# Weight signs through ScalarE's leaky slope, the first loads on one queue, and the big chunks' softmax and maxima spread over three blocks

## The chip, the cores and the metric

The kernel runs on one core of a Trainium2 chip. The metric is the device time of one execution, in microseconds (us). The engines are named as in the profile: PE (TensorE), PEld (its weight loads), DVE (VectorE), ACT (ScalarE), POOL (GpSimd), SP (the queue from which most transfers are issued; SPq and ACTq are the issuing sequencers of SP and ACT).

## What is computed

```python
w = softmax(weight_gen)                      # (4, 4096, 8 heads, 7 taps)
x_pad = 6 rows of zeros ahead of x           # x is (4, 4096, 192)
out = einsum('bshk,bskhg->bshg', w, x_unf)   # 7 taps of x, weighted per head
x = out.reshape(16384, 192)
h = x @ w_in                                 # w_in (192, 2048), float64
g = h * (1.0 / (1.0 + np.exp(-h)))
return (g @ w_out).astype(np.float32)        # w_out (2048, 192), float64
```

## The kernel before

Each of 128 partitions holds 128 consecutive tokens; four of them (TB) from every partition make a **block** of 512 tokens, so there are 32 blocks, 0 to 31. x and weight_gen come in **chunks** of 1, 1, 2 and then seven times 4 blocks; chunks 3 to 9, the big ones, begin at blocks 4, 8, ..., 28. For a block the seven taps are multiplied and added (`prep_steps`, L418 and L424, on DVE with a share on POOL), split into two float16 halves `xs` (L393 on ACT, L396 on DVE), transposed by a DMA into `xt` (L403) and copied with the two halves of the partitions swapped into `xu` (L388). Then come two products: `mm1` (L509) makes `h` for a pair of 128 columns of w_in at a time, ACT applies silu and makes the upper half of `g` (L521, L522), DVE the lower half (L527, `lower`), and `mm2` (L541) adds to `acc`. Eight pairs make a block. `mm1` runs three pairs ahead of `mm2`; four buffers hold `h`, so `mm1` of a pair waits until DVE has finished `lower` of the pair two before.

Before a chunk can be used, its weights need the softmax (`softmax_steps`: row maxima `wm` L318, subtraction L321 on POOL, exp L325 on ACT, row sums `ws` L329, their reciprocal L333 and L334, product L337 on POOL) and x needs the largest magnitude of the chunk, from which its float16 scale is taken (`scale_steps`: up to four partial maxima `xm` L351, their maximum `m_x` L157, a write of 128 values to DRAM, `d_x` L160, and a read back to all partitions, `mb_x` L161, `ra_x` L166 and the small scales).

Blocks 0 and 1 are an opening of its own. Block 0 runs in float32: its seven products are added up on PE (L455), turned on PE (L471), and `mm1` (L497) and `mm2` (L550) use the weights as float32. w_in and w_out arrive as pairs of 32-bit words (`raw`, nine buffers) and are turned to float32 in 8 + 8 pieces I0 to I7 and O0 to O7 (`convert_steps`): `move` (L211, ACT) shifts the exponent of the upper words, `sign` (L173 and L216, DVE) puts together the sign bit and the three bits of the lower words, and `join` (L220, DVE) combines them. `size` (L225, ACT) takes each piece's sum of magnitudes; the largest of the sums (`w_scale_steps`: L254 on DVE, a product on PE L257, L260 on DVE, a product L264) sets the weights' float16 scale, with which `upper_w` (L238) and `lower_w` (L242) make the float16 halves that block 1 is the first to use. The scale of block 1's x goes through PE (`x1_all`, L647, L660, L661), that of blocks 2 and 3 (chunk 2) through `x2_size` (L666) and `d_x`, `mb_x` on SP; `z2` is the step that reads them.

The order of all this is a table. `OPENING` has for each of the first 16 pairs three lists of steps (before `mm1`; after it; inside the `mm2` that follows): S, J stand for `sign`, `join` of an I piece and G, Q of an O piece, I and O for `move`, B and D for `size`, U, L, P, R for `upper_w` and `lower_w`, M and A for block 1's products and sums, X for its split and transpose, Wr, Wa, Wb, Wc for the weights' scale. `START` has the units at which the later steps are issued: a block has 16 units, two for each pair, and `chain` counts from two blocks before the block or chunk in question. DVE, ACT, PE and SP each execute in the order that results.

```python
    "any_s": (3, 3, 7, 9, 9, 9),
    "any_x": (1, 5, 6.5, 9, 9.5, 19.75, 19.75, 20.5),
    "any_v": (12, 13, 15, 19, 20, 20.75, 21.5, 22.25, 24.5, 25, 25),
```

Of the kernel before, what the change touches and what calls it, by code (L numbers as in the profile page):

```python
# [52 lines left out]
    "chunk2": (2.5,),  # L53
# [16 lines left out]
def kernel(  # L70
# [77 lines left out]
    def absmax_by_dma(m, name, queue=nc.sync):  # L148
# [20 lines left out]
        return got, [rows, over]  # L169
# [33 lines left out]
    wsum = const.tile([P, 2, NP], F32, name="wsum")  # L203

    def convert_steps(kind, p):
# [17 lines left out]
        def size():  # L223
            junk = sm_p.tile([P, 2 * D], mybir.dt.bfloat16, tag="junk", name=f"junk{kind}{p}", bufs=1)
            nc.scalar.activation(out=junk, in_=v, func=AF.Abs, accum_out=wsum[:, col, p:p + 1])  # L225

        return [move, sign, join, size]
# [46 lines left out]
    def load_x(c):  # L274
# [4 lines left out]
        if t0 == 0:  # L279
# [5 lines left out]
            nc.scalar.dma_start(out=t[1:1 + cut, 0:HALO, :], in_=xf[0:cut, T - HALO:T, :])  # L285
            nc.scalar.dma_start(out=t[1 + cut:P, 0:HALO, :], in_=xf[cut:P - 1, T - HALO:T, :])
# [312 lines left out]
    with tc.manual_schedule():  # L599
        load_w(0)  # L600
        load_x(0)
        load_w(1, nc.scalar)
        load_w(2, nc.scalar)
# [5 lines left out]
        load_x(1)  # L609
        load_piece("I", 1)  # L610
# [68 lines left out]
        step |= {"y": lambda: x_scales({"all": px[:, P:P + 1]}, 1), "x2": x2_size, "n2": lambda: (tot2(), rec2(), norm2()), "n1": lambda: (tot1(), rec1(), norm1()),  # L679
                 "Wr": w_rows, "Wa": w_turn, "Wb": w_over, "Wc": w_scale}  # L680
        for p in range(NP):
            for kind, names in (("I", "ISJ" "B" "UL"), ("O", "OGQ" "D" "PR")):
                steps = conv[kind, p] + [lambda k=kind, p=p: upper_w(k, p), lambda k=kind, p=p: lower_w(k, p)]
                step.update({f"{n}{p}": f for n, f in zip(names, steps)})
        for n in ("I0", "S0", "J0"):
            step.pop(n)

        for c in range(2, NC):
# [8 lines left out]
            def prepare(c=c, u0=u0):  # L697
# [122 lines left out]
```

## Time and profile before

| what | value |
|---|---|
| median of 3 runs | 1084.42 us (1084.2 to 1084.54) |
| the profiled execution | 1084.3 us, its span 1082.5 us |
| PE | 1049.9 us busy, 97% of the span |
| DVE, ACT | 784.7 us (72%), 775.0 us (72%) |
| POOL | 293.2 us (27%) |
| chain that ended last | PE 77%, DVE 9%, ACT 6%, DMA 5%, issue 3% |

The profile covers one execution. A busy share is a mean over stages that have different limits, so the table alone doesn't say where time can be won: a stage's waits do. Times of the span count from its start.

### The profile page before, as it was taken

How to read it: one execution, taken by the hardware profiler on the slowest of the kernel's cores; microseconds unless marked ns; L12 is line 12 of the kernel's file. 1: busy time of each engine (PE TensorE's matmuls, PEld its weight loads, DVE VectorE, ACT ScalarE, POOL GpSimd, SP SyncE). 2: the span in 40 equal slices, each digit the busy share in tenths (PEclk: the TensorE clock that was granted, in tenths of full speed). 3: DMA queues.
4: the chain of work that ended last, by engine and by line, in shares of the span. 5: the costliest groups of instructions: out<-in, count | busy, mean ns of one | idle time of the engine just before them, and what ended most of it. 6: DMA issues, size and time to landing. Idle time of an engine off the chain costs nothing.

```text
span 1082.5 us, 36860 instructions
## 1 busy us (share of the span) xinstructions
PE 1049.9 (97%) x16472; PEld 811.3 (75%) x16472; DVE 784.7 (72%) x1134; ACT 775.0 (72%) x1264; POOL 293.2 (27%) x169
## 2 busy tenths in 40 slices
PE   6988999999999999999999998999999999999998
PEld 4655677777777777777777776777777777777776
DVE  6888886678866697677867686667886669767643
ACT  3765777678777777777767785767877777777775
POOL 1000343331513343312433304333151334331100
PEclk9999999999999999999999999999999999999999
DMA  8412132111411115111331104111131111211110
GB/s 214 139 30 118 42 133 50 39 45 32 131 46 45 39 38 145 32 31 46 91 85 46 46 19 142 39 39 46 31 131 46 45 38 40 48 31 32 45 46 16
DMA packets 73790, 67.71 MB, mean 63 GB/s; under 512 B 52639, under 2 KB 67103, under 8 KB 72606
## 3 DMA queue, kind: packets, MB, share of 16 engines
q1 hardware_dynamic: 73184, 64.43, 21.8%
q8 instruction: 128, 2.10, 0.9%
q10 hardware_dynamic: 446, 0.93, 0.3%
q14 instruction: 32, 0.26, 0.1%
HBM read 28.37 MB, written 12.59 MB: 38 GB/s over the span
## 4 chain that ended last, share of the span: by engine, by line
PE 77%; DVE 9%; ACT 6%; DMA 5%; issue 3%; SPq 0%; DVEq 0%; ACTq 0%
PE h L509 37%; PE acc L541 37%; DVE pr L424 2%; ACT h L521 2%; DVE g L527 1%; PE acc L554 1%; DVE pr L418 1%; DMA xc<-in_x_dram 1%; DMA xu<-xt 1%; DMA xt<-xs 1%; DVE xm L351 1%; ACT g L522 1%; DMA d_x<-xs 1%; PE sum L455 1%; PE h L497 1%
## 5 line engine op out<-in xcount | busy, mean ns | idle before, releaser
L527 DVE SCALAR_TENSOR_TENSOR g<-h,gup,g 128x512 f16<-128x512 f32 x496 | 369.0, 747 | 264.8 <-ACT g L522 264.4
L541 PE MATMUL acc<-wo,g 64*128 64x192 f16 x11424 | 556.6, 243 | 0.0
L541 PEld LDWEIGHTS <-g 64*128 64x128 f16 x11424 | 528.5, 94 | 25.2 <-issue 0.2
L521 ACT ACTIVATE h<-h,inv 128x512 f32<-128x512 f32 x496 | 326.5, 658 | 251.0 <-PE h L509 250.2
L509 PEld LDWEIGHTS <-w 64*128 64x128 f16 x4464 | 278.7, 94 | 203.4 <-issue 24.0
L522 ACT ACTIVATE g<-h,gup 128x512 f16<-128x512 f32 x496 | 341.0, 687 | 16.2
L509 PE MATMUL h<-xt,w 64*128 64x512 f16 x2232 | 310.7, 376 | 10.8 <-DVE g L527 10.8
L509 PE MATMUL h<-xu,w 64*128 64x512 f16 x2232 | 308.8, 377 | 4.3 <-DMA xu<-xt 4.3
L418 POOL TENSOR_TENSOR pr<-xc,wc 128x768 f32<-128x768 f32 x87 | 144.4, 1674 | 507.5 <-DVE pr L424 407.2
L418 DVE TENSOR_TENSOR pr<-xc,wc 128x768 f32<-128x768 f32 x130 | 130.9, 1008 | 0.0
L424 DVE TENSOR_TENSOR pr<-pr,pr 128x768 f32<-128x768 f32 x128 | 130.1, 1016 | 0.3
L424 POOL TENSOR_TENSOR pr<-pr,pr 128x768 f32<-128x768 f32 x58 | 122.2, 2107 | 4.5
L575 DVE SCALAR_TENSOR_TENSOR o<-acc,od,t 128x192 f32<-128x192 f32 x120 | 44.1, 408 | 3.5 <-ACT t L574 3.5
L574 ACT ACTIVATE t<-acc,od 128x192 f32<-128x192 f32 x120 | 43.6, 418 | 3.8 <-PE acc L554 3.8
L321 POOL TENSOR_TENSOR wc<-wc,wm 128x896 f32<-128x896 f32 x7 | 12.3, 1757 | 107.6 <-DVE wm L318 107.6
L396 DVE SCALAR_TENSOR_TENSOR xs<-pr,xup,xs 128x768 f16<-128x768 f32 x31 | 35.3, 1138 | 6.4 <-ACT xs L393 4.3
L337 POOL TENSOR_TENSOR wc<-wc,ws 128x896 f32<-128x896 f32 x7 | 12.3, 1754 | 89.6 <-DVE ws L334 89.6
L393 ACT ACTIVATE xs<-pr,xup 128x768 f16<-128x768 f32 x31 | 28.7, 925 | 9.1 <-DVE pr L424 9.1
L351 DVE TENSOR_REDUCE xm<-xc 128x1 f32<-128x960 f32 (+1 forms) x28 | 34.4, 1228 | 0.0
L550 PEld LDWEIGHTS acc<-v_out,g 128*128 128x128 f32 x128 | 21.4, 196 | 4.9 <-issue 1.8
L550 PE MATMUL acc<-v_out,g 128*128 128x192 f32 x128 | 24.3, 344 | 0.0
L554 PEld LDWEIGHTS <-g 128*128 128x128 f16 x240 | 20.1, 100 | 5.4 <-issue 5.1
(87 smaller groups left out, 254.6 us busy)
## 6 DMA issues: line engine op xcount, KB each, us to landing
xc<-in_x_dram SPq DMA_DIRECT2D x7, 2112.0 KB, 10.4
xu<-xt SPq DMA_DIRECT2D x62, 192.0 KB, 2.8
out_dram<-o SPq DMA_DIRECT2D x58, 192.0 KB, 1.9
wc<-in_weight_gen_dram SPq DMA_DIRECT2D x7, 448.0 KB, 6.4
rawI<-in_moe_w_in_dram SPq DMA_DIRECT2D x16, 192.0 KB, 6.5
rawO<-in_moe_w_out_dram SPq DMA_DIRECT2D x8, 384.0 KB, 4.3
xc<-in_x_dram SPq DMA_DIRECT2D x1, 1344.0 KB
xc<-in_x_dram SPq DMA_DIRECT2D x2, 384.0 KB, 6.0
```

The lines of the kernel that those rows point to most:

```text
L351: nc.vector.tensor_reduce(out=m[:, i:i + 1], in_=x_t[c][:, cuts[i]:cuts[i + 1], :].rearrange("p t d -> p (t d)"), op=ALU.max, axis=AX.X, a ...
L396: nc.vector.scalar_tensor_tensor(out=xs[:, ts, D:2 * D], in0=acc, scalar=sc[c, "up"], in1=xs[:, ts, 0:D], op0=ALU.mult, op1=ALU.subtract)
L418: eng.tensor_tensor(out=pr[k].rearrange("p t (h g) -> p (t h) g", g=G), in0=xin, in1=wv, op=ALU.mult)
L424: eng.tensor_tensor(out=pr[k], in0=pr[k], in1=pr[l], op=ALU.add)
L509: nc.tensor.matmul(h_t[b, p + NP * i], w16[rows, g, part, p * P:(p + 1) * P], x_in[rows, :, k, :], start=n == 0, stop=n == NT9 - 1)
L521: nc.scalar.activation(out=h, in_=h, func=AF.Silu, scale=sc[c, "inv"])
L522: nc.scalar.activation(out=gh, in_=h, func=AF.Copy, scale=sc[c, "gup"])
L527: nc.vector.scalar_tensor_tensor(out=gl_t[b, f], in0=h, scalar=sc[chunk_of[b], "gup"], in1=gh_t[b, f], op0=ALU.mult, op1=ALU.subtract)
L541: nc.tensor.matmul(acc_t[b, i, t // 2][:, t % 2, :], g[rows, t * P:(t + 1) * P], wo16[rows, f, part], start=f == ORDER[0] and t % 2 == 0 a ...
L550: nc.tensor.matmul(acc_t[b, 0, t // 2][:, t % 2, :], gh_t[b, f][:, t * P:(t + 1) * P], v_out[:, f % NP, f // NP], start=f == 0 and t % 2 = ...
L574: nc.scalar.activation(out=t1, in_=a[0], func=AF.Copy, scale=sc[c, "od"])
L575: nc.vector.scalar_tensor_tensor(out=o[:, t, :], in0=a[1], scalar=sc[c, "od"], in1=t1, op0=ALU.mult, op1=ALU.add)
```

## The change

- `move` uses ACT's leaky slope (Prelu) in place of a copy: for negative values the slope of -2^32 raises the exponent by 32, and after the shift by three bits in `join` that is the sign bit. So `sign` shrinks to `rest`, one instruction (L174 in the new numbering), and the instruction at L216 is gone, once for each of 16 pieces.
- `size_w` takes the magnitudes of two pieces at once: eight instructions of 768 elements in place of 16 of 384.
- The rows of x ahead of block 0 and the weights of chunks 1 and 2 are loaded by SP's queue, not ACT's, in the order w of chunk 0, x of chunk 0, rows ahead, w of chunk 1, piece I0, x of chunk 1, w of chunk 2.
- Softmax of chunks 1 and 2 goes in between block 0's products; the scales of block 1 and of chunk 2 go through DRAM by POOL's queue, each a `d_x` and an `mb_x`, and `z2` moves from the 11th to the 14th pair.
- `Wa`, the product on PE that needs all sizes, moves from inside `mm2` of pair 3 to after it; `n1`, M and A move to earlier pairs.
- From chunk 4 on, the chunk's softmax and maxima begin up to 40 units earlier than before and lie in three blocks; chunk 3 has lists of its own.

```diff
 OPENING = (
...
-    ("I7 O6 B3", "O7 D2 D3 B4 B5 S6 J6 G4 Q4 G5 Q5 M5 A5", ""),
-    ("B6 D4", "D5 B7 S7 J7 G6 Q6 G7 Q7 M4 A4", ""),
-    ("", "D6 D7 Wr M3 A3", "Wa M2 A2"),
-    ("Wb M1 A1 M0 A0 X", "Wc U0 L0 U1 U2 P0 L1", "L2 U3 R0 P1 L3"),
+    ("I7 O6", "O7 B1 D1 B2 S6 J6 G4 Q4 G5 Q5 M4 A4 y", "M3 A3"),
+    ("D2", "S7 J7 G6 Q6 G7 Q7 B3 M2 A2", ""),
+    ("", "D3 M1 A1 Wr M0 A0 X", ""),
+    ("Wa", "Wb", "Wc U0 U1 P0 L0 L1"),
...
-    "any_s": (3, 3, 7, 9, 9, 9),
-    "any_x": (1, 5, 6.5, 9, 9.5, 19.75, 19.75, 20.5),
+    "first_s": (1, 1, 5, 8, 9, 9),
+    "first_x": (0, 3, 6, 11, 11.25, 15, 21, 21, 22),
+    "any_s": (-32, -32, -21, -15.5, -14.5, -14.5),
+    "any_x": (-38, -30.5, -22, -6, -5, 0, 4, 4, 5),
+    "early": (-40,),
...
         def move():
-            nc.scalar.activation(out=v, in_=raws[kind, p][..., 1].bitcast(F32), func=AF.Copy, scale=REBIAS)
-
-        def sign():
-            low, high = raws[kind, p][..., 0], raws[kind, p][..., 1]
-            bits(t, low, 29, ALU.logical_shift_right)
-            nc.vector.scalar_tensor_tensor(out=t, in0=high, scalar=SIGN, in1=t,
-                                           op0=ALU.bitwise_and, op1=ALU.bitwise_or)
+            nc.scalar.activation(out=v, in_=raws[kind, p][..., 1].bitcast(F32), func=AF.Prelu, scale=REBIAS,
+                                 alpha=TO_BIT_31)
+
+        def rest():
+            bits(t, raws[kind, p][..., 0], 29, ALU.logical_shift_right)
...
-            nc.scalar.dma_start(out=t[1:1 + cut, 0:HALO, :], in_=xf[0:cut, T - HALO:T, :])
-            nc.scalar.dma_start(out=t[1 + cut:P, 0:HALO, :], in_=xf[cut:P - 1, T - HALO:T, :])
+            nc.sync.dma_start(out=t[1:1 + cut, 0:HALO, :], in_=xf[0:cut, T - HALO:T, :])
+            nc.sync.dma_start(out=t[1 + cut:P, 0:HALO, :], in_=xf[cut:P - 1, T - HALO:T, :])
...
-        load_w(1, nc.scalar)
-        load_w(2, nc.scalar)
+        load_w(1)
...
-        px = ps_o.tile([P, 2, D], F32, tag="acc", name="x1_all").rearrange("p a d -> p (a d)")
+        got1, (rows_1, spread1, over1) = absmax_by_dma(xs1, "x1", nc.gpsimd)
+        rows_1()
+        spread1()
...
-            got, (rows, over) = absmax_by_dma(xs2, "x2")
+            got, (rows, spread, over) = absmax_by_dma(xs2, "x2", nc.gpsimd)
             rows()
+            spread()
```

The start of ACT's program. Before, four transfers are issued ahead of the first table load (`xc` is x, `wc` the softmax weights, the number is the buffer's):

```order
L285 DMA xc_114<-in_x_dram 112x1152
L286 DMA xc_114<-in_x_dram 15x1152
L307 DMA wc_119<-in_weight_gen_dram 128x224
L307 DMA wc_121<-in_weight_gen_dram 128x448
L623 ACT_TABLE_LOAD
L623 ACTIVATE warm<-ones 1x1
L325 ACTIVATE wc_112<-wc_112 128x224
```

Now:

```order
L625 ACT_TABLE_LOAD
L625 ACTIVATE warm<-ones 1x1
L327 ACTIVATE wc_112<-wc_112 128x224
L296 ACTIVATE xc_114<-zero 1x1152
L327 ACTIVATE wc_119<-wc_119 128x224
```

The four transfers have left ACT's order; they are in SP's, and ACT begins with its table.

DVE in the opening, up to the maximum of the weights' sizes (`w_rows`), which PE's `Wa` waits for. Before, the last pieces and three of block 1's sums (`pr`) stand ahead of it, each piece with three instructions:

```order
L173 TENSOR_SCALAR tI_304<-rawI_165 128x384
L216 SCALAR_TENSOR_TENSOR tI_304<-rawI_165,tI_304 128x384
L220 SCALAR_TENSOR_TENSOR v_in<-v_in,tI_304 128x384
L173 TENSOR_SCALAR tO_311<-rawO_170 128x384
L216 SCALAR_TENSOR_TENSOR tO_311<-rawO_170,tO_311 128x384
L220 SCALAR_TENSOR_TENSOR v_out<-v_out,tO_311 128x384
...
L418 TENSOR_TENSOR pr_2_352<-xc_114,wc_119 128x768
L424 TENSOR_TENSOR pr_0_350<-pr_0_350,pr_2_352 128x768
L254 TENSOR_REDUCE w_rows<-wsum 128x2
```

Now:

```order
L174 TENSOR_SCALAR tI_295<-rawI_165 128x384
L219 SCALAR_TENSOR_TENSOR v_in<-v_in,tI_295 128x384
L174 TENSOR_SCALAR tO_302<-rawO_170 128x384
L219 SCALAR_TENSOR_TENSOR v_out<-v_out,tO_302 128x384
L174 TENSOR_SCALAR tO_303<-rawO_172 128x384
L219 SCALAR_TENSOR_TENSOR v_out<-v_out,tO_303 128x384
L420 TENSOR_TENSOR pr_4_354<-xc_114,wc_119 128x768
L426 TENSOR_TENSOR pr_0_350<-pr_0_350,pr_4_354 128x768
L420 TENSOR_TENSOR pr_5_355<-xc_114,wc_119 128x768
L426 TENSOR_TENSOR pr_0_350<-pr_0_350,pr_5_355 128x768
L256 TENSOR_REDUCE w_rows<-wsum 128x2
```

A piece has two instructions, and three more of block 1's products with their sums (taps 3, 4 and 5) stand ahead of `w_rows`.

DVE around the split `xs` of a block in the stage where a chunk is made ready. Before, the row sums `ws`, their reciprocal and the last partial maximum `xm` follow the split at once:

```order
L527 SCALAR_TENSOR_TENSOR g_12_6768<-h_12_6745,gup_4635,g_12_6768 128x512
L396 SCALAR_TENSOR_TENSOR xs_5703<-pr_3_5699,xup_4625,xs_5703 128x4x192
L329 TENSOR_REDUCE ws_6779<-wc_4453 128x128
L333 TENSOR_SCALAR ws_6779<-ws_6779 128x128
L334 RECIPROCAL ws_6779<-ws_6779 128x128
L351 TENSOR_REDUCE xm_6432<-xc_4455 128x1
L527 SCALAR_TENSOR_TENSOR g_5_6853<-h_5_6833,gup_4635,g_5_6853 128x512
L157 TENSOR_REDUCE m_x_6857<-xm_6432 128x1
```

Now, in the block in which the last partial maximum is taken:

```order
L529 SCALAR_TENSOR_TENSOR g_12_6089<-h_12_6066,gup_3948,g_12_6089 128x512
L398 SCALAR_TENSOR_TENSOR xs_5021<-pr_3_5017,xup_3937,xs_5021 128x4x192
L529 SCALAR_TENSOR_TENSOR g_5_6168<-h_5_6148,gup_3948,g_5_6168 128x512
L353 TENSOR_REDUCE xm_4766<-xc_4440 128x1
L529 SCALAR_TENSOR_TENSOR g_13_6173<-h_13_6149,gup_3948,g_13_6173 128x512
L156 TENSOR_REDUCE m_x_6177<-xm_4766 128x1
L529 SCALAR_TENSOR_TENSOR g_6_6250<-h_6_6230,gup_3948,g_6_6250 128x512
```

Between the split and the next `lower` there is nothing any more; the sums and the reciprocal stand some eight pairs earlier, and the maximum two `lower` later.

## Rows read from the trace of the kernel before

**Rows 1.** The timeline of SP: start, length, what is issued, how often.

```profile
249.96 2.23 SPq L578 DMA_DIRECT2D out_dram<-o  x2
...
283.23 2.24 SPq L578 DMA_DIRECT2D out_dram<-o  x2
...
600.81 2.23 SPq L578 DMA_DIRECT2D out_dram<-o  x2
...
632.19 2.23 SPq L578 DMA_DIRECT2D out_dram<-o  x2
...
652.93 0.58 SPq L160 DMA_DIRECT2D d_x<-m_x  x1
...
670.14 2.24 SPq L578 DMA_DIRECT2D out_dram<-o  x2
...
891.69 2.23 SPq L578 DMA_DIRECT2D out_dram<-o  x2
...
924.96 2.23 SPq L578 DMA_DIRECT2D out_dram<-o  x2
```

**Rows 2.** The timeline of DVE, 640 to 658 us.

```profile
646.93 1.02 DVE L396 SCALAR_TENSOR_TENSOR xs<-pr,xup,xs 128x768 f16<-128x768 f32 x1
...
650.11 1.29 DVE L351 TENSOR_REDUCE xm<-xc 128x1 f32<-128x1152 f32 x1
```

**Rows 3.** The timeline of PE, 600 to 672 us; in brackets the idle time before, and its releaser.

```profile
652.11 0.37 PE L509 MATMUL h<-xt,w 64*128 64x512 f16 x1 [0.52 <-DVE g L527]
...
660.63 1.84 PE L509 MATMUL h<-xu,w 64*128 64x512 f16 x9 [2.83 <-DMA xu<-xt]
```

**Rows 4.** The view of the tile xu: all 62 transfers into it.

```profile
DMA to landing us min/median/max: 2.7/2.8/8.3
```

**Rows 5.** The timeline of ACT, 0 to 33 us.

```profile
1.91 4.32 ACTq L307 DMA_DIRECT2D wc<-in_weight_gen_dram  x2
6.26 1.28 ACT L623 ACT_TABLE_LOAD   x1 [6.26 <-DMA xc<-in_x_dram]
```

**Rows 6.** The timeline of DVE, 0 to 34 us.

```profile
8.07 0.39 DVE L329 TENSOR_REDUCE ws<-wc 128x32 f32<-128x224 f32 x1 [1.77 <-ACT wc L325]
...
19.19 0.96 DVE L460 TENSOR_TENSOR pr<-pr,pr 128x768 f32<-128x768 f32 x1
...
27.98 0.56 DVE L216 SCALAR_TENSOR_TENSOR tI<-rawI,tI 128x384 int32<-128x384 int32 x1
28.64 0.56 DVE L220 SCALAR_TENSOR_TENSOR v_in<-v_in,tI 128x384 int32<-128x384 int32 x1
```

**Rows 7.** The timeline of all engines, 0 to 45 us: PE's last sum and first product.

```profile
22.23 1.56 PE L455 MATMUL sum<-pr,ident 128*128 128x384 f32 x4
...
26.20 0.38 PE L661 MATMUL x_all<-r_x,ones 1*128 1x1 f32 x2 [0.84 <-DVE r_x L660]
...
26.51 8.01 PE L497 MATMUL h<-xv,v_in 64*128 64x256 f32 x48
```

**Rows 8.** The timeline of PE, 36 to 92 us.

```profile
51.17 1.57 PE L550 MATMUL acc<-v_out,g 128*128 128x192 f32 x8
56.34 0.38 PE L257 MATMUL w_all<-ident,w_rows 128*2 128x128 f32 x2 [3.60 <-DVE w_rows L254]
...
62.56 0.38 PE L264 MATMUL w_all<-w_diag,ones 2*128 2x2 f32 x2
...
73.56 1.24 PE L509 MATMUL h<-xu,w 64*128 64x512 f16 x9 [1.07 <-DMA xu<-xt]
```

**Rows 9.** The timeline of PE, 84 to 100 us.

```profile
84.60 2.15 PE L554 MATMUL acc<-wo,g 128*128 128x192 f16 x24
89.35 0.37 PE L509 MATMUL h<-xt,w 64*128 64x512 f16 x1 [2.60 <-DVE g L527]
...
95.75 1.25 PE L509 MATMUL h<-xt,w 64*128 64x512 f16 x9
```

**Rows 10.** The chain that ended last, 60 to 90 us: start, length, what.

```profile
73.25 8.98 DMA d_x<-xs
...
82.25 5.14 DMA mb_x<-d_x
```

More of the change, by code (lines that the diff above doesn't have):

```diff
@@ L52 @@
     "prep": (9.9,),
-    "chunk2": (2.5,),
     "load": (0,),
@@ L160, in rows, with spread @@
             queue.dma_start(out=d.unsqueeze(1), in_=m1)
-            queue.dma_start(out=mb, in_=d.partition_broadcast(P))
-            got["mb"] = mb
+            got["d"], got["mb"] = d, mb
+        def spread():
+            queue.dma_start(out=got["mb"], in_=got["d"].partition_broadcast(P))
         def over():
@@ L167, in over @@
             got["all"] = r
-        return got, [rows, over]
+        return got, [rows, spread, over]
     def bits(out, in0, scalar1, op0, scalar2=None, op1=None):
@@ L221, in join, with size_w @@
                                            op0=ALU.logical_shift_left, op1=ALU.bitwise_or)
[L223 to L227, printed above, removed]
+        return [move, rest, join]
+    def size_w(kind, q):
+        v = v_in if kind == "I" else v_out
+        v = v[:, 2 * q:2 * q + 2].rearrange("p q a n -> p (q a n)")
+        col = "IO".index(kind)
+        junk = sm_p.tile([P, 4 * D], mybir.dt.bfloat16, tag="junk", name=f"junk{kind}{q}", bufs=1)
+        nc.scalar.activation(out=junk, in_=v, func=AF.Abs, accum_out=wsum[:, col, q:q + 1])
     def halves_of(kind, p):
@@ L609 @@
         load_x(1)
+        load_w(2)
         load_piece("I", 1)
@@ L629 @@
         total(6, True, False)
-        for f in (top1, sub1, exp1, step.pop("zeros"), top2, sub2, exp2):
-            f()
-        nc.scalar.activation(out=warm[:, 1:2], in_=ones[0:1, 0:1], func=AF.Silu)
+        step.pop("zeros")()
+        between = {5: (top1, sub1, exp1), 4: (top2, sub2, exp2)}
         for k in range(5, 1, -1):
@@ L635 @@
             total(k, False, False)
+            for f in between.get(k, ()):
+                f()
+        nc.scalar.activation(out=warm[:, 1:2], in_=ones[0:1, 0:1], func=AF.Silu)
         xs1 = sm_p.tile([P, 1], F32, tag="xs1", name="xs1", bufs=1)
         xs2 = sm_p.tile([P, 1], F32, tag="xs2", name="xs2", bufs=1)
+        conv = {(k, p): convert_steps(k, p) for k in "IO" for p in range(NP)}
+        conv["I", 0][0]()
         rows1 = (HALO + TB) * D
@@ L677, in w_scale @@
             out_scale(1)
-        step |= {"y": lambda: x_scales({"all": px[:, P:P + 1]}, 1), "x2": x2_size, "n2": lambda: (tot2(), rec2(), norm2()), "n1": lambda: (tot1(), rec1(), norm1()),
+        step |= {"y": lambda: (over1(), x_scales(got1, 1)), "x2": x2_size, "n2": lambda: (tot2(), rec2(), norm2()), "n1": lambda: (tot1(), rec1(), norm1()),
                  "Wr": w_rows, "Wa": w_turn, "Wb": w_over, "Wc": w_scale}
         for p in range(NP):
-            for kind, names in (("I", "ISJ" "B" "UL"), ("O", "OGQ" "D" "PR")):
+            for kind, names in (("I", "ISJUL"), ("O", "OGQPR")):
                 steps = conv[kind, p] + [lambda k=kind, p=p: upper_w(k, p), lambda k=kind, p=p: lower_w(k, p)]
                 step.update({f"{n}{p}": f for n, f in zip(names, steps)})
+                if p % 2 == 0:
+                    step["BD"["IO".index(kind)] + str(p // 2)] = lambda k=kind, p=p: size_w(k, p // 2)
         for n in ("I0", "S0", "J0"):
@@ L700, in prepare @@
                 more.append(lambda: (finish_scales(c), out_scale(c)))
-                chain("any_s", steps, u0)
-                chain("any_x", parts + more, u0)
+                which = "any_" if chunks[c - 1][1] == CT else "first_"
+                chain(which + "s", steps, u0)
+                chain(which + "x", parts + more, u0)
             if c > 2:
-                at(u0, prepare)
+                at(u0 + (START["early"][0] if chunks[c - 1][1] == CT else 0), prepare)
         _, steps1, (hi1, lo1, turned1) = prep_steps(1, 0)
@@ L715, in prep @@
                 pool, steps, last = prep_steps(b, 0 if b == 2 else 3)
-                which = "b2" if b == 2 else "any_"
-                chain(which + "p", pool, u0)
-                chain(which + "v", steps + last, u0)
+                if b > 2:
+                    chain("any_p", pool, u0)
+                chain("b2v" if b == 2 else "any_v", steps + last, u0)
             at(START["prep"][0] if b == 2 else u0 - 1, prep)
```

15 lines of the change are left out of this document (4 added, 11 removed), and 14 rows, old and new, of the table OPENING.

## The prediction

> **What bounds the kernel now.** The table above has PE busy for 97% of the span, so outside its few gaps nothing can be won, and the question is where the gaps are. I read the page first, then PE's waits, then SP's timeline, since the store of a block's output marks the blocks.
>
> In the long run of equal blocks the reader is to see a period [rows 1]. From the store at 600.81 to that at 632.19 are 31.38 us, an undisturbed block of eight pairs at 3.92 us. In the block where a big chunk is made ready it is longer: 249.96 to 283.23 is 33.27, and the last of them, 891.69 to 924.96, is 33.27 again. There are six for chunks 4 to 9; five cost 1.89 us too much each, and the one from 632.19 to 670.14 costs 37.95 - 31.38 = 6.57. The cause of the 1.89 is on DVE [rows 2]: from the split at 646.93 to the end of the last partial maximum at 650.11 + 1.29 = 651.40 DVE does chunk work for 4.5 us, more than a pair's 3.92, and no `lower` comes in between. PE's next product then waits for `lower` [rows 3], 0.52 us in the row shown. The other 4.68 us of the odd block are a late `xu`: PE waits 2.83 us for it [rows 3] and runs slower for a while after. That transfer took 8.3 us where the median is 2.8 [rows 4], and `d_x` is issued right behind it, at 652.93 [rows 1].
>
> The opening is the other place. Call T0 the start of block 0's first product, 26.51 us [rows 7]. Ahead of T0 the path runs through softmax 0, seven products and their sums; DVE waits 1.77 us in it for exp [rows 6], because ACT first issues loads until 1.91 + 4.32 = 6.23 and only then loads its table [rows 5]. After T0, PE loses time at four places: 3.60 us waiting for `w_rows`, 1.07 for block 1's `xu` [rows 8], 2.60 for `lower` behind `z2` [rows 9], and the slower stretches after the long waits.
>
> **The start, -4.2.** (a) ACT no longer issues the four loads, so its table can be loaded long before the weights land. Of the 1.77 us only exp itself remains, about the 0.39 of the row sum of equal shape behind it [rows 6], plus a hand-over: 1.3 saved. (b) DVE is done with the products at 19.19 + 0.96 = 20.15 [rows 6], but PE's last sum starts at 22.23 [rows 7], 2.08 later, because PE is still busy with earlier sums. The product of tap 5 now precedes the softmax of chunks 1 and 2, so PE gets its sums spread out and should be up to date at the end: 2.08 saved. (c) The first product no longer stands behind the round trip of block 1's scale through PE, which waited 0.84 [rows 7]: 0.8 saved. The cost is on SP, which must issue four more transfers ahead of the weights. The nearest price is ACT's own issue row, two transfers in 4.32 us, the second of which waited for a landing; behind SP wait w of chunk 2 and pieces I1 onward, needed after T0 only. I add nothing for it. Bounds: 5.5 better if the first weights also land sooner, 0 if the rows ahead of block 0 land so late that tap 5 waits. The Trainium skill (DMA: Bandwidth & Descriptors, "Issuing engines are not separate DMA queues") says that issuing from several engines saves only sequencer time, usually small. By it alone (a) would be near 0 and the sum 1.3 smaller; the trace differs, since here ACT's sequencer was held for 5.5 us with a needed exp behind it.
>
> **The weights, -5.1.** From 51.17 to 62.56 [rows 8] are 11.39 us for a second product and a first product of block 0. At full rate they take 2 x 1.57 [rows 8] and 8.01 / 3 [rows 7], 5.8 together, so 5.6 are lost to `w_rows`. DVE reached it at about 56.1, T0 + 29.6. Ahead of it 15 pieces now lack the instruction that took 28.64 - 27.98 = 0.66 us of DVE [rows 6]: -9.9. Three more products and three sums, at about 0.95 as in the row at 19.19 [rows 6], stand ahead of it: +5.7. DVE will now sometimes outrun ACT, whose `move` of O0 stands behind the first silu: between 0 and 2, I take 2. So `w_rows` is ready at T0 + 27.4. PE comes to `Wa` after three first products (8.0) and seven more groups of about 2.8: T0 + 27.6. That is even; I leave 0.5 as a stall and count 5.1, bounds 3 and 5.6. `size_w` and the leaky slope lie on ACT, which waits for PE's products there, and I cost them at nothing; a leaky slope that is twice a copy would eat that cover on ACT, not on the path.
>
> **Block 1's xu, -1.1.** The split of block 1 ended on DVE about T0 + 39.7; by the same account it ends near T0 + 32. PE needs the swapped copy near T0 + 40, and from the split to it lie the transpose and a swap of 2.8 [rows 4], which I estimate at 7 together from the old 39.7 and the landing at 73.5, T0 + 47. So the 1.07 us wait [rows 8] goes, just. Bounds 0 and 1.4.
>
> **z2, -3.4.** From 84.60 to 95.75 [rows 9] are 11.15 us, against 2.15 + 2.1 + 2.1 at full rate: 4.9 lost, because DVE stands in `z2` until `mb_x` lands, at 82.25 + 5.14 [rows 10], and `lower` is queued behind. Now `z2` is issued three pairs, some 12 us, later. The chain itself (8.98 + 5.14 [rows 10]) starts near T0 + 43 and ends near T0 + 57; DVE comes to `z2` near T0 + 62. What is late next is DVE: seven products and six sums of block 2 at 0.95 with the lower halves of the weights fill these pairs, so I leave 1.5. Bounds 1 and 4.9.
>
> **The big chunks, -10.3.** The same steps remain, each now beside another pair. Of the 1.89 I leave 0.3 for the exp, which still needs two table loads of 1.28 [rows 5] in a row with it on ACT: six times 1.6, 9.6. Bounds: 0 left, or all 1.89. Chunk 3 has no room to spread, 0.7 for it (0 to 1.9). `d_x` stays right behind an `xu` in SP's order, that of the block before, so I keep one late `xu` in the sum: 0.
>
> **Sum.** 4.2 + 5.1 + 1.1 + 3.4 + 10.3 = 24.1. From the profiled execution's 1084.3 us (0.1 under the median of 1084.42) that gives 1060.2.
>
> **The rivals.**
> 1. No late `xu` at all: 4.7 less, 1055.5. For it: one of 62 was late [rows 4]. Chance 0.22.
> 2. The opening stays bound by DVE: `w_rows` and block 1's `lower` are as late as before, only start and `xu` are won. 24.1 - 8.5 = 15.6, so 1068.7. For it: the three extra products. Chance 0.13.
> 3. The chunk stalls move with the steps, because a lone step still pushes a `lower` over the slack: 0.3 won each in place of 1.6, 1068. Against it: a step alone is 1.1 to 1.3 us, under a pair's 3.92. Chance 0.10.
> 4. The round trip of `z2` on POOL's queue is slow. If it took twice 14.1 us it would end at T0 + 71, 9 us behind DVE, and give 1069; it matters from 5 us too much on. No row shows a transfer from POOL. The Trainium skill (SBUF — State Buffer, "SBUF: two separate sides") says that a transfer issued from POOL can wait for its descriptors while DVE runs a copy or scalar operation in its two-port mode, which speaks against this move; no run here shows it yet. Chance 0.05.
> 5. Slower: `d_x` holds back `xu` at every chunk. Each late `xu` costs about 6 us (4.68, and some 1.4 more, since the chunk's own stall hid a part of it and is gone), so from 1055.5 seven give 1097.5, and five already reach 1085.5. For it: DVE comes to `m_x` earlier, so `d_x` is always ready when `xu` is issued. Against it: one in seven before. Chance 0.02.
> 6. The leaky slope needs a table of its own, 32 loads of 1.28 [rows 5]: 41 us, 1101. Against it: both programs have 16 table loads. Chance 0.01.
>
> The forecast itself keeps 0.47.
>
> **Range and chances.** The lower end takes rival 1 and 3 us more from the start's and the opening's bounds: 1052.5. The upper end takes the opening's bounds (about 5 us worse) and half of the chunks' gain lost, or rivals 2 to 4: 1068.5. A measurement of this kernel can tell about 0.2%, 2.2 us. Faster by more than that: all cases but 5, 6 and several of 2 to 4 together, 0.96; same 0.01; slower 0.03.
>
> **What would show it.** Right: no L216 row; exp of chunk 0 within 0.5 us of its subtraction; the first product of block 0 near 22.3; PE's wait for `w_rows` under 1 us; no PE wait behind `z2`; stores 31.4 to 31.7 us apart in every block but at most one. Wrong: a first product after 25; a wait of 3 us or more at `w_all`; blocks of 33 us that now stand two or three blocks earlier; more than two `xu` landings above 5 us; a `d_x` from POOL that takes over 15 us.

## The result and the profile after

The changed kernel takes 1066.91 us (median of four runs, 1064.17 to 1069.1); before, the four runs beside it had a median of 1084.31. The ratio is 0.9845, 95% interval 0.9816 to 0.9874: faster by 17 us, where 24.1 were forecast. The profiled execution took 1066.89 us, its span 1064.9 against 1082.5 before. The terms missed in both directions, so they come first. Each is the difference of the same two marks in both traces: the first product of block 0 (T0), then the stores of the blocks.

| term | forecast | measured | marks, before and after |
|---|---|---|---|
| the start | 4.2 | 6.40 | T0 at 26.51 and 20.11 |
| the weights and block 1's `xu` | 5.1 + 1.1 | 1.97 | T0 to the store of block 0: 57.11 and 55.14 |
| `z2` | 3.4 | 4.94 | to the store of block 1: 39.49 and 34.55 |
| chunk 3 | 0.7 | -3.96 | to the store of block 2: 32.71 and 36.67 |
| chunks 4 to 9 | 9.6 | 8.25 | to the end of the span: 926.68 and 918.43 |
| sum | 24.1 | 17.60 | spans 1082.5 and 1064.9 |

The stores of blocks 0 to 2 on SP's timeline, before:

```profile
83.62 0.38 SPq L564 DMA_DIRECT2D out_dram<-o  x1
...
123.11 0.35 SPq L564 DMA_DIRECT2D out_dram<-o  x1
...
155.82 2.24 SPq L578 DMA_DIRECT2D out_dram<-o  x2
```

After:

```profile
75.25 0.35 SPq L566 DMA_DIRECT2D out_dram<-o  x1
...
109.80 0.35 SPq L566 DMA_DIRECT2D out_dram<-o  x1
...
146.47 2.24 SPq L580 DMA_DIRECT2D out_dram<-o  x2
```

The wait for block 1's `xu` stood at 73.56 [rows 8], ahead of the store of block 0, so it belongs to the second row. It is gone, and the weights alone won about 0.9 of the 5.1.

PE's waits over the whole span of the changed kernel (who waits, for whom: us in total, times, longest):

```profile
PE h L511 <- DMA xu<-xt: 6.6, 2, 3.7
PE w_all L259 <- DVE w_rows L256: 3.2, 1, 3.2
...
PE h L511 <- DVE g L529: 1.3, 2, 1.0
...
PE sum L457 <- DVE pr L462: 0.7, 1, 0.7
PE acc L543 <- DVE o L577: 0.6, 1, 0.6
```

The waits for `lower` (L529) are down to two, and none is left at the boundaries of chunks 4 to 9, where [rows 3] have one. Two waits for `xu` and the one for `w_rows` remain. With the slow stretches behind them they are most of what is missing.

DVE's timeline at the start (start, length, what, idle before it):

```profile
2.96 0.39 DVE L320 TENSOR_REDUCE wm<-wc 128x32 f32<-128x224 f32 x1 [1.96 <-DMA wc<-in_weight_gen_dram]
...
4.23 0.39 DVE L331 TENSOR_REDUCE ws<-wc 128x32 f32<-128x224 f32 x1 [0.46 <-ACT wc L327]
...
15.88 0.96 DVE L462 TENSOR_TENSOR pr<-pr,pr 128x768 f32<-128x768 f32 x1
```

PE's timeline behind it:

```profile
16.89 1.56 PE L457 MATMUL sum<-pr,ident 128*128 128x384 f32 x4 [0.69 <-DVE pr L462]
18.39 1.64 PE L473 MATMUL turn<-ident,xa 128*128 128x128 f32 x12
20.11 1.13 PE L499 MATMUL h<-xv,v_in 64*128 64x256 f32 x8
```

The wait for exp is 0.46, not 1.77 [rows 6], and the weights of chunk 0 are there at 2.96, 2.5 us sooner. PE takes its last sum at 16.89, right behind DVE's last product (16.84), where it came 2.08 late [rows 7].

The weights. ACT's timeline, 18 to 50 us, and PE's:

```profile
29.87 0.56 ACT L212 ACTIVATE v_in<-rawI 128x384 f32<-128x384 f32 x1 [3.06 <-DMA rawI<-in_moe_w_in_dram]
...
34.67 0.57 ACT L212 ACTIVATE v_out<-rawO 128x384 f32<-128x384 f32 x1 [1.19 <-DMA rawO<-in_moe_w_out_dram]
37.36 0.57 ACT L212 ACTIVATE v_out<-rawO 128x384 f32<-128x384 f32 x1 [2.12 <-DMA rawO<-in_moe_w_out_dram]
```

```profile
50.88 0.38 PE L259 MATMUL w_all<-ident,w_rows 128*2 128x128 f32 x2 [3.23 <-DVE w_rows L256]
51.19 4.54 PE L499 MATMUL h<-xv,v_in 64*128 64x512 f32 x12
```

No piece was late before. Now `move` waits for pieces that have not landed, and PE waits 3.23 for `w_rows`, nearly the 3.60 of before [rows 8]. The slow stretch behind the wait is there too (12 products in 4.54 us; undisturbed ones take 2.85): the granted clock from 50.90 to 55.70 is 0.64 of 2.4 GHz on the mean.

SP's timeline, stores and one chunk boundary:

```profile
460.71 2.24 SPq L580 DMA_DIRECT2D out_dram<-o  x2
...
493.31 2.23 SPq L580 DMA_DIRECT2D out_dram<-o  x2
...
587.58 2.23 SPq L580 DMA_DIRECT2D out_dram<-o  x2
...
607.90 0.58 SPq L159 DMA_DIRECT2D d_x<-m_x  x1
615.92 0.33 SPq L163 DMA_DIRECT2D mb_x<-d_x  x1
624.40 2.23 SPq L580 DMA_DIRECT2D out_dram<-o  x2
...
687.16 2.23 SPq L580 DMA_DIRECT2D out_dram<-o  x2
...
718.69 2.24 SPq L580 DMA_DIRECT2D out_dram<-o  x2
```

The block with a chunk's exp takes 31.53 us (687.16 to 718.69) in place of 33.27 [rows 1]: 1.74 won, six times. But from 587.58 to 624.40 are 36.82 us, 5.44 too many. One boundary earlier, a block of 32.60 (460.71 to 493.31) costs another 1.22. PE's clock at the long block (the stretch, its length, PE's busy time, the granted clock as a share of 2.4 GHz, the busy share of the DMA engines, GB/s):

```profile
600.00:611.00 11.00, 11.00 (x194) 1.00 0.44 73
615.00:619.00 4.00, 3.97 (x45) 0.60 0.07 14
619.00:623.00 4.00, 4.00 (x74) 1.00 0.02 6
```

PE waits 3.74 us for `xu`, and then the granted clock is 0.60 on the mean of 4 us (0.50, its lower level of 1.2 GHz, in the first three): 1.6 more. Together 5.3 of the 5.44.

### The profile page after: what moved, and what is told of

The parts are those of the page before. It is cut to its first block, busy times and chain, and to the rows that moved or that the text cites. A ratio compares the mean times of both kernels' runs of the same rounds, so it can differ in the third digit from the quotient of the medians.

```text
span 1064.9 us, 36830 instructions
## 1 busy us (share of the span) xinstructions
PE 1043.8 (98%) x16469; PEld 815.0 (77%) x16469; DVE 780.6 (73%) x1118; ACT 773.3 (73%) x1248; POOL 290.1 (27%) x173
## 4 chain that ended last, share of the span: by engine, by line
PE 88%; DMA 5%; DVE 4%; ACT 2%; issue 1%; SPq 0%; DVEq 0%; ACTq 0%
PE acc L543 44%; PE h L511 42%; DMA xu<-xt 1%; DMA rawI<-in_moe_w_in_dram 1%; PE acc L556 1%; DVE pr L420 1%; DMA xt<-xs 1%; DVE g L529 1%; PE h L499 1%; DMA rawO<-in_moe_w_out_dram 1%; DVE pr L426 1%; DMA xc<-in_x_dram 0%; ACT h L523 0%; PE acc L552 0%; ACT g L524 0%
## 5 line engine op out<-in xcount | busy, mean ns | idle before, releaser
L529 DVE SCALAR_TENSOR_TENSOR g<-h,gup,g 128x512 f16<-128x512 f32 x496 | 369.6, 747 | 255.9 <-ACT g L524 255.0
L511 PEld LDWEIGHTS <-w 64*128 64x128 f16 x4464 | 282.1, 94 | 186.9 <-issue 12.7
L420 POOL TENSOR_TENSOR pr<-xc,wc 128x768 f32<-128x768 f32 x87 | 135.8, 1576 | 453.6 <-DVE pr L426 435.9
L426 DVE TENSOR_TENSOR pr<-pr,pr 128x768 f32<-128x768 f32 x128 | 127.0, 993 | 0.3
L398 DVE SCALAR_TENSOR_TENSOR xs<-pr,xup,xs 128x768 f16<-128x768 f32 x31 | 46.3, 1492 | 3.9 <-ACT xs L395 1.9
L339 POOL TENSOR_TENSOR wc<-wc,ws 128x896 f32<-128x896 f32 x7 | 15.4, 2203 | 111.4 <-ACT h L523 93.4
L499 PE MATMUL h<-xv,v_in 64*128 64x512 f32 (+1 forms) x108 | 23.9, 587 | 0.1
```

What stands on the lines that cost most here:

```text
L398: nc.vector.scalar_tensor_tensor(out=xs[:, ts, D:2 * D], in0=acc, scalar=sc[c, "up"], in1=xs[:, ts, 0:D], op0=ALU.mult, op1=ALU.subtract)
L420: eng.tensor_tensor(out=pr[k].rearrange("p t (h g) -> p (t h) g", g=G), in0=xin, in1=wv, op=ALU.mult)
L426: eng.tensor_tensor(out=pr[k], in0=pr[k], in1=pr[l], op=ALU.add)
L511: nc.tensor.matmul(h_t[b, p + NP * i], w16[rows, g, part, p * P:(p + 1) * P], x_in[rows, :, k, :], start=n == 0, stop=n == NT9 - 1)
L529: nc.vector.scalar_tensor_tensor(out=gl_t[b, f], in0=h, scalar=sc[chunk_of[b], "gup"], in1=gh_t[b, f], op0=ALU.mult, op1=ALU.subtract)
```

## The theory

`d_x` writes 128 values of 4 bytes to DRAM. The theory is that, while such a write is under way, other transfers stand still or trickle: the pieces of the weights behind block 1's `d_x` (issued at 17.02), and an `xu` that has `d_x` right behind it. What the DMA engines moved in the changed kernel, 606 to 618 us, in 40 slices (busy tenths, GB/s), and the landings:

```profile
DMA  7000008987940000000000000000000004000000
GB/s 164 0 0 0 0 0 184 256 164 236 410 63 0 0 0 0 0 0 0 0 0 0 0 0 0 0 0 0 0 0 0 0 0 55 0 0 0 0 0 0
...
xu<-xt SPq DMA_DIRECT2D x2, 192.0 KB, 5.2
mb_x<-d_x SPq DMA_DIRECT2D x1, 64.0 KB, 4.1
d_x<-m_x SPq DMA_DIRECT2D x1, 0.5 KB, 8.0
```

The data of `xu` and `d_x` move in 1.8 us (slices 7 to 12). Then nothing moves for over 6 us, until `d_x` lands at 615.9; `xu` is told as landed only at 615.0. The same view of 24 to 32 us, when pieces of the weights are on the way:

```profile
DMA  9990900909009391330799112004283680614989
GB/s 79 31 33 20 26 0 0 15 23 26 0 10 41 74 77 18 67 31 5 59 51 61 46 46 13 0 10 54 100 69 79 72 72 36 36 59 102 120 72 136
DMA packets 310, 0.37 MB, mean 47 GB/s; under 512 B 20, under 2 KB 310, under 8 KB 310
```

The mean is 47 GB/s, until block 1's `d_x` lands, 14.3 us after its issue. The rivals: the nine raw buffers come free too late; it is POOL's queue; something else delays `xu`; and, for what the change itself brought, that a part of it is worth nothing.

## The experiments

**1. The sign by DVE again.**

```diff
-    ... func=AF.Prelu, scale=REBIAS, alpha=TO_BIT_31)
+    ... func=AF.Copy, scale=REBIAS)
     bits(t, raws[kind, p][..., 0], 29, ALU.logical_shift_right)
+    nc.vector.scalar_tensor_tensor(out=t, in0=raws[kind, p][..., 1], scalar=SIGN, in1=t,
+                                   op0=ALU.bitwise_and, op1=ALU.bitwise_or)
```

> The changed kernel with one part undone: move is a copy again and DVE puts the sign in by a second instruction, in each of 16 pieces. Theory: DVE's order is what w_rows waits for, so 15 instructions of 0.5 to 0.66 us ahead of it, less some 2 us that DVE now idles for pieces that have not landed, make w_rows 5.5 to 8 us later, and the time 5 to 8 us longer (1072 to 1075); PE's wait for w_rows goes from 3.2 to 8 us or more. Rival: after the change the pieces' landing sets w_rows (DVE idled 1.8 and 2.0 us for them), so the second instruction fits beside that: w_rows under 2 us later, time within 2 us of the changed kernel's.

Measured: 1072.02 us, ratio to before 0.9904 (0.9883 to 0.9925), 0.6% or 6.4 us above the change's ratio. DVE comes to `w_rows` at T0 + 35.6 in place of T0 + 30.6, and PE's waits begin with

```profile
PE w_all L261 <- DVE w_rows L258: 8.3, 1, 8.3
```

The time fits the theory, and `w_rows` is 5.1 us later, just under its 5.5: even with pieces that land late, DVE's order decides, and the slope is worth 5 us on the path. On ACT it costs what the copy did (0.55 us each in both kernels).

**2. The first loads on ACT's queue.**

```diff
-            nc.sync.dma_start(out=t[1:1 + cut, 0:HALO, :], ...)
-            nc.sync.dma_start(out=t[1 + cut:P, 0:HALO, :], ...)
+            nc.scalar.dma_start(out=t[1:1 + cut, 0:HALO, :], ...)
+            nc.scalar.dma_start(out=t[1 + cut:P, 0:HALO, :], ...)
...
-        load_w(1)
+        load_w(1, nc.scalar)
+        load_w(2, nc.scalar)
```

> The changed kernel with the rows ahead of block 0 and the weights of chunks 1 and 2 issued from ACT's queue again. Theory: the start's gain of 6.4 us is made of 2.5 us by which w of chunk 0 lands earlier (2.96 against 5.48), 1.0 of ACT being ready for exp, and 2.9 of the two other steps, so this kernel's first product moves from 20.11 back to about 23.5, and the time is 3 to 4 us longer. Rival (what issues a load does not matter, only that softmax of chunks 1 and 2 moved behind the products): first product within 0.5 us of 20.1, time within 1.5 us.

Measured: T0 at 23.43 as expected (DVE has w of chunk 0 at 5.26 only, exp starts at 7.62), but 1064.15 us, ratio 0.9836 (0.9819 to 0.9853): no slower than the change. T0 to the store of block 0 is 51.22 us here and 55.14 there: what the start lost, the wait for `w_rows` gave back (1.0). The two expectations failed each in one half. An earlier T0 bought nothing in that state: for 3.3 us of T0 the last piece that ACT waits for came 1.7 earlier (37.36 against 39.06) and `w_rows` 1.1, and the slow stretch behind the longer wait took the rest.

**3. Block 1's maximum by PE, with no write to DRAM.**

```diff
-        got1, (rows_1, spread1, over1) = absmax_by_dma(xs1, "x1", nc.gpsimd)
-        rows_1()
-        spread1()
...
-        nc.tensor.matmul(spare[:, 0:P], ident16, ident16, start=True, stop=True)
+        nc.tensor.matmul(spare[0:1, 0:P], xs1, ident, start=True, stop=True)
...
+            nc.vector.tensor_reduce(out=x1r, in_=spare[0:1, 0:P], op=ALU.max, axis=AX.X)
+            nc.tensor.matmul(spare[:, P:P + 1], ones[0:1], x1r, start=True, stop=True)
```

> The changed kernel with the maximum of block 1's x taken across partitions by PE, as before the change, in place of the write to DRAM and the read back; the second product of it stands one pair later than before. Theory: the write of 128 values of 4 bytes (issued at 17.0, landed 14.3 us later) holds up the pieces of the weights that share the engines: the transfers move 270 GB/s until 23 us and 40 to 110 GB/s from 23 to 33. Without it a piece lands within 9 us of its issue (14.0 at most now), ACT and DVE no longer wait for pieces, PE's wait for w_rows falls from 3.2 to under 1 us, and the time by 3 to 4 us. Rival: the nine raw buffers come free too late (their release follows the first product), so the gap in the stream stays, w_rows waits 2.5 to 3.2, and the time is within 1 us.

Measured: 1052.19 us (1051.99 to 1053.2), ratio 0.9724 (0.9709 to 0.9739). Pieces land within 8.0 us, neither ACT nor DVE waits for one, PE's wait for `w_rows` is gone, and T0 to the store of block 0 is 51.41. That is the theory, and the buffers are out. But the time is 13 us lower by the ratios where 3 to 4 were expected. Of the 14.9 us between the two spans 11 lie behind block 0: no `xu` was late (longest landing 4.8), though `d_x` stands right behind it as before. Experiments 11 and 12 ask why.

**4. The same write from ACT's queue.**

```diff
-        got1, ... = absmax_by_dma(xs1, "x1", nc.gpsimd)
+        got1, ... = absmax_by_dma(xs1, "x1", nc.scalar)
```

> The changed kernel with the same write and read back for block 1's x, but issued from ACT's queue in place of POOL's, the read back two pairs later. If writes of 4 bytes hold up the stream whatever issues them: gap, wait for w_rows and time as in the changed kernel, within 1.5 us. If it is POOL's queue: as the kernel in which PE takes the maximum, 3 to 4 us less. If neither (the buffers): as the changed kernel, and the PE version too.

Measured: 1062.9 us, ratio 0.9816 (0.9795 to 0.9838), 3 us below the change by the ratios, which by itself is the time expected if POOL's queue were the cause. The marks say otherwise: a `w_rows` wait of 4.8 and T0 to the store 56.63; between 24 and 32 us the engines moved 0.46 MB, and SP issues no piece from 20.1 to 29.3, when the write lands. What makes it faster lies behind the opening: chunk 3's `xu` is not late here (its block takes 32.02 us in place of 36.67) and the later blocks lose 2.5 us less. The write holds up the weights from this queue as well: POOL's queue is not the cause.

**5. `d_x` away from `xu`.**

```diff
-    "first_x": (0, 3, 6, 11, 11.25, 15, 21, 21, 22),
-    "any_x": (-38, -30.5, -22, -6, -5, 0, 4, 4, 5),
+    "first_x": (0, 3, 6, 11, 15, 19, 23, 23, 24),
+    "any_x": (-38, -30.5, -22, -6, 0, 6, 11, 11, 12),
```

> The changed kernel with one number changed per step: the write d_x of a chunk's maxima is issued 5 units (3.75 for chunk 3) later, so no longer right behind the two transfers into xu, and the read back and the scales follow later too. Theory: xu is late where d_x stands right behind it (7.7 and 7.2 us in the changed kernel, 8.3 before, each time about 1 us before d_x itself lands), so no xu takes over 5 us any more, PE's waits for xu (3.7 and 2.9) go, as does the block that is 1.2 us long because a scale's read back came late, and the time falls by 8 to 11 us. Rival: what delays xu is not d_x (the transpose, loads, instruction fetches): one or two xu of 7 to 8 us remain, time within 3 us of the changed kernel's.

Measured: 1056.32 us (1054.75 to 1061.76), ratio 0.977 (0.974 to 0.9799), 8 us better by the ratios. No `xu` over 4.8. A new loss stands in PE's waits: "issue" (PE waits for nothing that the profile names), 2.3 us, at block 3, in which chunk 3's `d_x` is written. The profiled execution is the slowest of the four, by over 5 us, so its losses are not those of every execution of this program.

**6. More such writes.**

```diff
             swapped(b, slice(0, TB), (nc.sync, nc.sync))
+            if b >= 7 and b % 4 != 2:
+                d = dr_p.tile([P], F32, tag="more", name=f"more{b}")
+                nc.sync.dma_start(out=d.unsqueeze(1), in_=zero)
```

> The changed kernel with a further write of 128 values of 4 bytes to DRAM, of no use, right behind xu in 19 of the blocks that have none. Theory: each makes xu late with the share seen so far (3 of 14 boundaries in the two traces), at 4.5 to 5.5 us each: about 4 late blocks more, 15 to 30 us longer, and each late xu has landed in the same 1 to 2 us as the write behind it. Rival: late xu have nothing to do with the write: at most 2 in the whole trace, time within 3 us of the changed kernel's.

Measured: 1082.06 us (1075.72 to 1089.31, ten runs), ratio 1.0 (0.9977 to 1.0023): 15 to 17 us lost, all that the change had won. PE's waits:

```profile
PE h L514 <- DMA xu<-xt: 13.6, 4, 5.8
PE h L514 <- issue: 7.7, 3, 3.7
```

Four waits for `xu`, two more than in the change where the theory had about four more, and three waits of another kind. So a write doesn't always hurt, and it seems to have a second way to: PE waits for nothing that the profile names. The three end at 265.81, 399.70 and 656.88, each in a block where such a write (at 256.73, 384.47 and 641.98) has the next chunk's loads right behind it; five of the 19 stand so.

**7. The chunks' steps where they were.**

```diff
-    "any_s": (-32, -32, -21, -15.5, -14.5, -14.5),
-    "any_x": (-38, -30.5, -22, -6, -5, 0, 4, 4, 5),
-    "early": (-40,),
+    "any_s": (3, 3, 7, 9, 9, 9),
+    "any_x": (1, 5, 6.5, 9, 9.5, 9.5, 19.75, 19.75, 20.5),
+    "early": (0,),
```

(`first_s` and `first_x` likewise.)

> The changed kernel with the chunks' softmax and maxima at the units they had before. Theory: each of six boundaries is 1.7 us longer again (33.27 against 31.53), 10 us in all; with as many late xu as the changed kernel has, 1077; with one less, 1072. Rival: the spread is worth nothing by itself, the stalls only having moved: within 3 us of the changed kernel's.

Measured: 1067.3 us, ratio 0.987 (0.9849 to 0.9892), and the time alone would say that the spread is worth nothing. The stores say otherwise:

```profile
236.94 2.23 SPq L580 DMA_DIRECT2D out_dram<-o  x2
...
270.21 2.23 SPq L580 DMA_DIRECT2D out_dram<-o  x2
...
301.59 2.23 SPq L580 DMA_DIRECT2D out_dram<-o  x2
```

33.27 us again in all six boundaries, 10.4 in all, as expected; the time misses the 1072 to 1077. For here no `xu` of a later chunk was late, where the changed kernel lost 5.44 and 1.22 there, chunk 3's cost PE 1.8, not 2.9 (its block 2.0 less), and T0 to the store of block 0 is 2.2 less. 10.4 lost and 10.9 won met.

**8. Experiments 3 and 5 together.** Both edits as shown there.

> Both mends at once: block 1's maximum by PE and d_x away from xu. Theory: the two gains add, 11 to 15 us below the changed kernel, 1052 to 1056. Rival: the gain at the weights is taken back by DVE's work for block 1, so the sum is that of d_x alone, about 1058.

Measured: 1055.02 us (1054.71 to 1055.52), ratio 0.9749 (0.9735 to 0.9764): inside the range for the sum, yet 2.7 us above PE alone by the ratios. T0 to the store of block 0 is 51.41; what is lost stands in block 3:

```profile
PE acc L543 <- issue: 2.3, 1, 2.3
```

There `d_x` has the next chunk's loads right behind it. The DMA view of 131.8 to 146 us:

```profile
q1 hardware_dynamic: 358, 1.64, 77.8%
issues: line engine op xcount, KB each, median us to landing
xc<-in_x_dram SPq DMA_DIRECT2D x1, 2112.0 KB, 16.5
...
d_x<-m_x SPq DMA_DIRECT2D x1, 0.5 KB, 7.3
```

No row of the instruction queue (q8) stands in it, while the view of 606 to 618 us in the changed kernel has one packet there in 12 us. With PE's "issue" behind it (146.3 to 148.6; `d_x` landed at 140.5) I read this as PE's instructions arriving late; the trace does not show which packet was for which engine, nor whether the write or the loads behind it held them up.

**9. The 128 values gathered in SBUF, then written in one run.**

```diff
-            queue.dma_start(out=d.unsqueeze(1), in_=m1)
+            g = sm_p.tile([1, P], F32, tag="dg", name=f"dg_{name}")
+            queue.dma_start(out=g.rearrange("a (p e) -> a p e", e=1), in_=m1)
+            queue.dma_start(out=d.unsqueeze(0), in_=g)
```

> The changed kernel with each d_x made in two steps: the 128 values are first gathered into one partition by a transfer within SBUF, and then written to DRAM in one run of 512 bytes. Everything else stays, POOL's queue for block 1's too. Theory: it is the 128 writes of 4 bytes to DRAM that stop the other transfers. Without them the weights' stream has no gap at 24 to 32 us (wait for w_rows under 1 us), no xu lands later than 5 us, and the time is 10 to 14 us below the changed kernel's: 1053 to 1057. Rival 1: any transfer of 128 times 4 bytes does it, in SBUF too: late xu and the gap stay, time within 3 us. Rival 2: it is POOL's queue for the gap: no late xu, but w_rows waits 3 us as now, about 1056 to 1059.

Measured: 1052.13 us (1051.63 to 1052.93), ratio 0.9725 (0.9707 to 0.9742). The same window as above, 24 to 32 us, with POOL's queue still in use:

```profile
DMA  9999999958999955569999999889999899988999
...
DMA packets 1733, 2.08 MB, mean 260 GB/s; under 512 B 148, under 2 KB 1732, under 8 KB 1732
```

260 GB/s in place of 47. PE's wait for `w_rows` is 1.1, T0 to the store 51.25, and the transfers into `xu`:

```profile
DMA to landing us min/median/max: 2.7/3.0/4.7
```

One edit removes the gap and the late `xu`, and neither rival stands. For the gap, that shows the writes of 4 bytes to DRAM as the cause. For the late `xu` one edit is not enough, since experiment 3 keeps the writes of chunks 3 to 9 and has none late. All runs together show it: in the four programs with no such write right behind `xu` (5, 8, 9 and 10) none is late, and of the programs with one, all but that of experiments 3 and 12 have at least one late. The chain is also shorter: for chunks 3 to 9 SP issues the read back 3.7 us (median) after the gathering, and it takes 2.8, where the changed kernel's write and read back took 8.0 and 4.4.

**10. Experiments 3 and 9 together.** Both edits as shown there.

> The same two steps for d_x, and block 1's maximum by PE. Theory: the path to the first product and the weights is that of the kernel with PE alone, and no transfer of the chunks can hold anything up, so the time is that of the kernel with PE alone, 1052, within 1 us, whatever the writes would have done. Rival: the two transfers in place of one cost SP or the read back something: 1 to 3 us more, seen as a wait for ra_x on DVE.

Measured: 1052.09 us (1051.48 to 1053.09), ratio 0.9725 (0.9707 to 0.9742). As expected; no wait for `ra_x`.

**11. The kernel of experiment 3, with `d_x` elsewhere in DRAM.**

```diff
-            d = dr_p.tile([P], F32, tag="d", name=f"d_{name}")
+            d = dr_p.tile([16 * P], F32, tag="d", name=f"d_{name}")[0:P]
```

> The kernel with block 1's maximum by PE, but each d_x in DRAM lies 8 KB from the next in place of 4 KB, so that nearly all lie elsewhere; no instruction differs. It asks why that kernel had no late xu at all although d_x stands right behind xu in it as before. Theory 1: where in DRAM the write goes decides: one or two late xu, and 1056 to 1063. Theory 2: it is the timing against the other transfers, which is unchanged here: no late xu, 1052 within 1 us.

Measured: 1063.36 us (1062.56 to 1064.85), ratio 0.9832 (0.981 to 0.9855). Not one instruction differs in kind or place, and PE waits again:

```profile
PE h L511 <- DMA xu<-xt: 7.1, 2, 4.3
```

Theory 1: between these two programs the place in DRAM decides whether the write hurts, at a cost of 10 us against experiment 12 on the same chip. What about the place it is stays open; neither the trace nor these runs show it. Nor is the place all of it: the kernel before has the same eight `d_x` at the same distance as experiment 3, and there chunk 7's `xu` was late. Before, in the change and in experiments 1, 2, 4, 7 and 11 the late ones are always those of chunks 3 and 7.

**12. The kernel of experiment 3 once more, on another chip.**

> The kernel with block 1's maximum by PE once more, on another chip. If the absence of late xu belongs to the program: 1052 within 1 us and no xu over 5 us. If it was chance: one or two late xu, 1056 to 1063.

Measured: 1053.21 us (1051.91 to 1054.91), ratio 0.9735 (0.9715 to 0.9755), longest `xu` 4.3. That is a little more than 1 us above 1052, but no `xu` is late: its absence belongs to the program, not to chance. T0 alone was 23.27 in the profiled execution (first x and rows ahead landed later), T0 to the store 51.42 again.

The opening over all profiles, T0 to the store of block 0:

| write for block 1's x | T0 to store, us |
|---|---|
| before (none, through PE) | 57.11 |
| 4 bytes each, opening as in the change | 55.14, 56.81 (5), 51.25 (6), 52.94 (7) |
| the same from ACT; with loads on ACT | 56.63 (4); 51.22 (2) |
| none, or one run of 512 bytes | 51.41 (3), 51.41 (8), 51.25 (9), 51.42 (10), 51.42 (11), 51.42 (12) |

Programs whose opening is alike spread over 5.6 us with the write, and those without it over 0.2. So with the write the loss goes from nothing to 5.6 us. In experiment 6 the stream between 24 and 32 us was slow too (70 GB/s), but DVE waited for no piece, where it waits 2.0 us for one in the changed kernel.

## Why the prediction was right, and where not

The forecast of 1060.2 was 6.7 us too low; its range, to 1068.5, held 1066.9. That it held is in part luck: two losses that were not costed, 4.2 us at the weights and 4.7 at chunk 3, met gains of 2.2 at the start and 1.5 at `z2` beyond the forecast. Of the signs of error that it names one came, a wait of 3 us at `w_all`, and it points at the right step.

**The start: mechanism right, size off.** (b) and (c) came as put: from DVE's last product to T0 are 3.27 us against 6.36, 3.1 won of 2.9 forecast. (a) was sized 1.3 and is 3.3 (16.84 against 20.15). The wait for exp fell by the 1.3 forecast. What I missed is that w of chunk 0 lands 2.2 us after its issue when SP's loads go one behind the other, and 4.5 to 4.7 when ACT's go beside them (experiment 2 and before). I had it only in the bound. The rule that I weighed there (the Trainium skill, DMA: Bandwidth & Descriptors, "Issuing engines are not separate DMA queues") would put (a) near 0; it prices the issue, and here most of (a) came from the order of landing.

**The weights: the step that failed is the landing of the pieces, which I did not cost.** I counted DVE's instructions (confirmed by experiment 1) and got w_rows at T0 + 27.4; it came at T0 + 30.6. Without block 1's write it comes at T0 + 28.2 (3) or 28.4 (9), the 57.11 fall to 51.4, and the term with block 1's `xu` is 5.7 where I said 6.2. I had looked at POOL's round trip only where it sat on the path (rival 4, `z2`) and never at what the one of block 1 would do to transfers beside it. Rival 2's time (1068.7) is near the result, but its mechanism, DVE's three extra products, is not what happened.

**Block 1's xu and z2: right in the mechanism.** The wait for `xu` is gone, as forecast. `z2` won 4.94 for 3.4: the 1.5 that I left for DVE is not lost. DVE reads the scale with no wait, and POOL's `d_x` took 7.8 us where SP's had taken 8.98 [rows 10]. Rival 4 is out.

**Chunk 3: the second step that failed, a late xu that I put at nothing.** Its `d_x` stands behind `xu` too, and the boundary lost 3.96 in place of winning 0.7. With no late `xu` (3) block 2 takes 32.02 us, 0.7 less than before, as forecast.

**The big chunks: right, and one late xu kept, right.** 1.74 each for 1.6. The late one cost 5.44 for 4.68 before, close to the "about 6" that I put on one whose cover is gone, and 1.22 more went at the block that ends at 493.31, behind a `d_x` that took 9.85 us. Experiments 3 and 9 have 31.4 us there. No `xu` is late in it: ACT's silu stands idle for 2.48 us, where 1.27 is usual, and begins at 490.46, 0.2 after that `d_x` has landed; what held it the profile does not show. Rival 5 (all boundaries) needed five late ones to be slower; I weighed it by one case in seven; experiment 6 has four late ones and three of PE's other waits in 26 writes. The executions of 3, 11 and 12 agree within 3 us each; but those of experiment 6 spread over 13.6 us and those of experiment 5 over 7.

The page that bears on the cause gives 512 bytes as the least size for full rate and says that below it a transfer is a read-modify-write (the Trainium skill, DMA: Bandwidth & Descriptors, "Specifications"). The traces agree that such a write is slow: 128 times 4 bytes take 7 to 10 us to land in the changed kernel's chunks; no run shows a read-modify-write. Its section "Back-pressure in remote DMA" says of transfers between cores that stalled writes stall the other queues of the same DMA engine. Here other queues' transfers were held up within one core, by writes from the queues of SP, ACT and POOL alike; that it is the same mechanism no run shows.

## What to carry to other kernels

Do not send one small value per partition to DRAM while other transfers matter: gather within SBUF first, or let PE turn the column into a row; here the gathering was worth 13 us by the ratios and made, with PE or without, the fastest kernels (1052.1, 30 us below before). When a step moves to another queue, cost what its transfers do to the others beside it, not only when it lands. And read a change by its marks rather than by its total: in experiment 7 a loss of 10.4 us and gains of 10.9 hid each other.

## What was not expected of the hardware

- A write of 128 times 4 bytes to DRAM, half a kilobyte, cut the stream of the weights from 260 to 47 GB/s for 8 us, from POOL's queue and much the same from ACT's (57). In the other programs with it the same stretch has 62 to 121.
- Whether it hurts can depend on where in DRAM it goes: 4 KB or 8 KB from one to the next made 1053.2 and 1063.4 us of one and the same order of instructions. Why is open.
- One load was there after 2.2 us or 4.7 us, by whether another queue had loads going at the same time.
